# GpSimd's sums of exponentials added head by head, in an attention kernel with a mixture of experts

## The chip, the cores and the metric

The kernel runs on one core of a Trainium2 chip. The metric is the device time of one execution, in microseconds. The core has five engines that the text names: TensorE (PE in the profile; PEld is its loading of weights), VectorE (DVE), ScalarE (ACT), GpSimd (POOL) and SyncE (SP, which here only issues DMAs). Each takes its own instructions strictly in order, and semaphores hold an instruction until what it needs is there.

## What is computed

Attention with a capped score, in float32, over 8 batches, 12 heads, 448 positions and 64 columns a head. Then each of the 3584 tokens goes to one of 8 experts, of which each keeps the 80 tokens with the largest gate weight:

```python
scores = cap * np.tanh(scale * np.matmul(q, k.transpose(0, 1, 3, 2)) / cap)
attn = np.exp(scores - scores.max(-1, keepdims=True))
attn = attn / (attn.sum(-1, keepdims=True) + 1e-09)
x = np.matmul(attn, v)                      # -> (3584, 768)
expert_idx = np.argmax(x @ w_gate, axis=1)  # gate_w: its softmax probability
# per expert e: the `capacity` tokens of largest gate_w
out[tok] = gate_w[tok, None] * (np.maximum(x[tok] @ w1[e], 0.0) @ w2[e])
```

## The kernel before

The attention loop takes the heads in pairs, 48 of them (6 a batch). The scores of a pair lie with the 448 keys on partitions, in chunks of 128, and the 448 queries along the free axis. `qk` (L1033) multiplies a chunk for both heads into a PSUM tile sc (L1047) and ScalarE takes its tanh into the tile e (L1055). `expo` (L1057) takes the exponential in place (L1060). `av` (L1066) multiplies the exponentials with the values (L1071), four heads at a time; L1090 and L1100 add the 64 keys that are left over.

The denominator needs the sum of the exponentials over the keys. `esum` (L1103), the function that is changed, adds chunks on GpSimd: L1108 adds the second chunk to the first for both heads, 896 columns, into the tile t1 (the trace calls it t), and L1110 adds the third. `sums` (L1112) then lets TensorE sum over the partitions: in a group of two pairs, four matmuls read t (L1117) and four read the keys left over (L1118), into the PSUM tile sp. VectorE transposes sp (L1121, into st), adds a guard (L1123), takes the reciprocal (L1124) and spreads it (L1126, into r). `scaled` (L1129) multiplies av by r into x (L1133), which frees av's PSUM bank for the next group. `turned` (L1135) transposes x into xb (L1141), which GpSimd's queue stores once a batch (L1147). `swap` (L1074) exchanges the halves of the left-over keys (L1082).

The order is written out by hand: the strings EVEN, ODD, NEXT and LAST (L52 to L55) name the steps of a pair. q is `qk`, x and y are `expo` with `esum` right behind it, a is `av`, u is `sums`, n is `scaled`, m is `turned`, w is `swap`. At each b the function `background` (L1237) puts in some of the gate's and the ranking's work, which is mostly VectorE's, by costs that are written beside each piece. None of these costs or strings is touched.

The names in the background work that matter here: `gate_math` (L283) finds each token's expert and its key, with w at L322 and g at L336; `ranks` (L392) compares the keys of all tokens, with gb at L425 (L420 in the end), gl at L411, and the TensorE sums pd (L432), which VectorE adds into dfc (L438) and so frees a PSUM bank of the tag misc that sp shares. `prune` (L524) keeps the first candidates after five batches, with r at L543, us at L559, prlh at L566, prov at L573 and prrh at L576. `order` (L242), the other function that is changed, puts the experts that have tokens first: o1 makes a key, o4 the list as integers, from which SyncE later takes the addresses of the weights. `one` (L238) is tensor_scalar in the form that also writes out a sum, here into a place that nobody reads.

Behind the loop the tokens chosen are fetched and go through six experts (L779), while SyncE loads the weights (L767) into buffers, most of which lie where the loop's tiles were.

Of the kernel before, what the change touches and what calls it, by code (L numbers as in the profile page):

```python
# [12 lines left out]
ALU = mybir.AluOpType  # L13
# [21 lines left out]
NPRE = 4  # L35
# [86 lines left out]
def attn_moe(ctx, tc, q2, k, v, cap, wg, w1, w2, capacity, ct, out):  # L122
    nc = tc.nc
# [25 lines left out]
    def cst(key, n=128):  # L149
        a, b = CT[key]  # L150
        return ctt[:n, a:b]
# [24 lines left out]
    ev = consts.tile([128, E], F32, name="ev")  # L176
    ev0_i = consts.tile([1, NPRE], I32, name="ev0_i")
# [10 lines left out]
    neso = consts.tile([128, E], F32, name="neso")  # L188
# [43 lines left out]
    def wide(a, n=E):  # L232
        return a.rearrange("p (a e) -> p a e", a=1).broadcast_to([a.shape[0], n, E])

    def deep(a, n=E):
        return a.rearrange("p (e a) -> p e a", a=1).broadcast_to([a.shape[0], E, n])

    def one(dst, src, s=0.0, op=ALU.add):  # L238

        nc.vector.tensor_scalar(dst, src, s, 0.0, op0=op, op1=ALU.add, accum_out=dump[:dst.shape[0]])  # L240

    def order(sm):  # L242

        key = sm.tile([128, E], F32, name="okey", tag="okey")
        pos = sm.tile([128, E], F32, name="opos", tag="opos")
        pm = sm.tile([128, E, E], F32, name="opm", tag="opm")

        def o1():
            nc.vector.tensor_scalar(key, neso, 0.0, 8.0, op0=ALU.is_equal, op1=ALU.mult)
            nc.vector.tensor_tensor(key, key, cst("io"), op=ALU.add)  # L250

        def o2():
            t = sm.tile([128, E, E], F32, name="ocmp", tag="ocmp")
            nc.vector.tensor_tensor(t, wide(key), deep(key), op=ALU.is_lt)
            nc.vector.tensor_reduce(pos, t, axis=AX.X, op=ALU.add)
            nc.vector.tensor_tensor(pm, wide(pos), deep(cst("io")), op=ALU.is_equal)

        def o3(dst, key):
            t = sm.tile([128, E, E], F32, name="ocmp2", tag="ocmp")
            nc.vector.tensor_tensor(t, pm, wide(key), op=ALU.mult)  # L260
            nc.vector.tensor_reduce(dst, t, axis=AX.X, op=ALU.add)

        def o4():
            nc.vector.tensor_copy(ev0_i, ev[0:1, 0:NPRE])
            nc.vector.tensor_scalar(rev, ev, -1.0, float(E), op0=ALU.mult, op1=ALU.add)
            nc.vector.tensor_tensor(gtv, wide(ev), deep(ev), op=ALU.is_gt)
            st["ordered"] = True
        return [o1, o2] + [lambda d=d, k=k: o3(d, k) for d, k in ((ev, cst("io")), (powv, cst("pow")), (nesk, neso))] + [o4]
# [726 lines left out]
    with ExitStack() as a2:  # L995
# [107 lines left out]
        def esum(p, i):  # L1103
            s = st[p]
            e = s["e"]
            if i == 0:
                t1 = s["es"] = sm.tile([CK, 2, S], F32, name=f"t1{p}", tag="t1", bufs=3)
                nc.gpsimd.tensor_tensor(t1, e[:, 0:2], e[:, 2:4], op=ALU.add)  # L1108
            else:
                nc.gpsimd.tensor_tensor(s["es"], s["es"], e[:, 4:6], op=ALU.add)  # L1110

        def sums(u):  # L1112

# [185 lines left out]
        for t in range(n + 1):  # L1299
# [12 lines left out]
            if 1:  # L1312
# [3 lines left out]
                for i, x in enumerate(todo):  # L1316
# [3 lines left out]
                    if k_ == 'q' and t < n:  # L1320
                        qk(t, a_)
                    elif k_ == 'q' and t == n:
                        begin()
                    elif k_ == 'x' and t < n:
                        expo(t, 0, 2)
                        esum(t, 0)
                    elif k_ == 'y' and 1 <= t <= n:
                        expo(t - 1, 2, 4)
                        esum(t - 1, 1)
                    elif k_ == 'a' and 2 <= t < n + 2:  # L1330
                        av((t - 2) // 2, int(x[1]), int(x[2]))
                    elif k_ == 'w' and t >= 2:
                        swap(t // 2 - 1)
                    elif k_ == 'l' and t >= 3:
                        av_late((t - 3) // 2 if t < n else (n - 2) // 2)
                    elif k_ == 'u' and (t % 2 and 3 <= t < n or t == n):
                        sums((t - 2) // 2)
                    elif k_ == 'n' and 3 <= t:
                        for f in range(2):
                            scaled((t - 3) // 2 if t < n else (n - 2) // 2, f)  # L1340
                    elif k_ == 'm' and t >= 4:
                        normed((t - 4) // 2)
                    elif k_ == 'b' and t < n + 2:
                        share = sum(c for c, _, _ in bg + urgent) / (PLACES * (left - 1) + todo[i:].count('b'))
                        share += sum(c for c, _, _ in low) / max(1, PLACES * (n - 2 - t))
                        background(min(max(share, 600), 2200 if t < LATER else 3500 if t < n else 4500), 0, SLACK[t >= LATER][t % 2][todo[:i].count('b')] if t < n else TAIL)
# [146 lines left out]
```

## Time and profile before

| | us |
|---|---|
| runs | 496.76 (median), 493.79, 499.2 |
| profiled execution, time | 499.33 |
| profiled execution, span of the trace | 497.5 |
| TensorE busy | 462.9 (93%) |
| ScalarE busy | 343.9 (69%) |
| VectorE busy | 281.7 (57%) |
| GpSimd busy | 263.1 (53%) |
| GpSimd's additions at L1108, 48 | 101.2 |
| GpSimd's additions at L1110, 48 | 101.0 |

The span runs from the first to the last instruction of the program; the time has 1.8 us around it. The granted clock of TensorE is 0.985 of full speed over the span. The loop takes about the first 377 us. An idle time in brackets behind an instruction is that of its engine just before it, with what ended it by the profile; where several semaphores are waited for, the profile names the one that came last among those it can see.

### The profile page before, as it was taken

The numbers are of one execution on the slowest core, as the hardware profiler recorded it, in microseconds if no ns is written. First come the engines' busy times: TensorE is split into PE (matmuls) and PEld (weight loads), VectorE is DVE, ScalarE is ACT, GpSimd is POOL, SyncE is SP. The second block draws the span as 40 slices with busy tenths as digits, with TensorE's granted clock in tenths as the row PEclk, the third lists the DMA queues.
The fourth block names the chain that finished last, engine by engine and source line by source line (L and its number), as shares of the span: only waits on it lengthen the run. The fifth ranks groups of instructions, "written<-read, shape, count | busy, mean of one in ns | idle before, by whom it ended". The sixth has DMA issues, their size and how long they took to land.

```text
span 497.5 us, 15023 instructions
## 1 busy us (share of the span) xinstructions
PE 462.9 (93%) x6188; PEld 208.0 (42%) x6188; DVE 281.7 (57%) x772; ACT 343.9 (69%) x370; POOL 263.1 (53%) x201
## 2 busy tenths in 40 slices
PE   6899999999989999989999989989999889979894
PEld 1122232232323332323333323324336778878793
DVE  1144447837784686498569938895676523433000
ACT  4999989989978997896888857885964044601111
POOL 1666676666557656565755673566494237224001
PEclk9999999999999999999999989999999989899998
DMA  5557478758737875753676475578269999999901
GB/s 152 150 155 214 115 187 226 217 149 231 165 83 185 209 220 151 173 159 112 167 204 165 119 209 135 127 201 219 65 189 376 343 393 387 319 352 349 347 8 48
DMA packets 68111, 99.14 MB, mean 199 GB/s; under 512 B 19232, under 2 KB 53056, under 8 KB 68032
## 3 DMA queue, kind: packets, MB, share of 16 engines
q1 hardware_dynamic: 63360, 83.82, 55.6%
q0 software_dynamic: 4672, 14.26, 11.3%
q8 instruction: 51, 0.84, 0.7%
q14 instruction: 28, 0.23, 0.1%
HBM read 74.54 MB, written 23.51 MB: 197 GB/s over the span
## 4 chain that ended last, share of the span: by engine, by line
PE 83%; DVE 8%; issue 3%; ACT 3%; POOL 1%; DMA 1%; SPq 0%; POOLq 0%; DVEq 0%; ACTq 0%
PE sc L1047 22%; PE av L1071 21%; PE hp L779 9%; PE yt L779 8%; PE sp L1117 4%; PE sp L1118 3%; PE sc L1054 3%; PE av L1100 3%; PE lgp L1160 3%; PE av L1090 2%; PE pd L432 2%; ACT e L1055 2%; ACT e L1060 1%; DVE gl L411 1%; PE yp L800 1%
## 5 line engine op out<-in xcount | busy, mean ns | idle before, releaser
L1055 ACT ACTIVATE e<-sc,scl 128x896 f32<-128x896 f32 x168 | 161.7, 1007 | 57.3 <-PE sc L1047 55.5
L1060 ACT ACTIVATE e<-e,capt 128x1792 f32<-128x1792 f32 x96 | 153.8, 1603 | 0.0
L1108 POOL TENSOR_TENSOR t<-e 128x896 f32<-128x896 f32 x48 | 101.2, 2109 | 89.2 <-ACT e L1060 89.1
L1047 PE MATMUL sc<-qt,kt 64*64 64x448 f32 x1152 | 134.4, 563 | 7.1 <-DMA qt<-in_q_dram 4.7
L1071 PE MATMUL av<-e,vr 128*32 128x448 f32 x1152 | 132.4, 545 | 4.1 <-DVE x L1133 4.1
L1110 POOL TENSOR_TENSOR t<-t,e 128x896 f32<-128x896 f32 x48 | 101.0, 2103 | 57.2 <-ACT e L1060 49.0
L1047 PEld LDWEIGHTS sc<-qt,kt 64*64 64x64 f32 x1152 | 35.7, 134 | 89.8 <-ACT e L1055 40.0
L1071 PEld LDWEIGHTS av<-e,vr 128*32 128x32 f32 x1152 | 33.3, 109 | 81.3 <-issue 62.1
L779 PE MATMUL yt<-thv,w 128*64 128x80 f32 x1152 | 45.3, 237 | 6.5 <-issue 6.5
L779 PE MATMUL hp<-xt,w 128*64 128x80 f32 x1152 | 45.5, 239 | 5.8 <-issue 5.0
L1082 DVE TENSOR_SCALAR_CACHE_REDUCE sw<-e 64x896 f32<-64x896 f32 x32 | 34.6, 1080 | 25.3 <-ACT e L1060 24.9
L779 PEld LDWEIGHTS hp<-xt,w 128*64 128x64 f32 x1152 | 42.8, 141 | 8.7 <-issue 7.4
L779 PEld LDWEIGHTS yt<-thv,w 128*64 128x64 f32 x1152 | 42.7, 140 | 8.0 <-issue 7.6
L1121 DVE STREAM_TRANSPOSE st<-sp 128x448 f32<-128x448 f32 x24 | 15.5, 648 | 53.4 <-PE sp L1118 53.3
L1133 DVE TENSOR_TENSOR x<-av,r 128x448 f32<-128x448 f32 x48 | 27.9, 619 | 22.9 <-PE av L1100 21.0
L425 DVE TENSOR_SCALAR_CACHE_REDUCE gb<-krow,kc 112x896 bf16<-112x896 f32 (+8 forms) x37 | 31.8, 882 | 0.0
L823 POOL DMA_INDIRECT out_dram<-ysv,si x6 | 5.7, 944 | 45.7 <-ACT ysv L822 32.3
L423 ACT ACTIVATE gz<-gb 112x896 bf16<-112x896 bf16 (+12 forms) x22 | 18.5, 844 | 13.8 <-DVE gb L420 13.7
L1141 DVE STREAM_TRANSPOSE xb<-x 128x448 f32<-128x448 f32 x48 | 27.9, 619 | 0.0
L1117 PE MATMUL sp<-t,ones 128*32 128x448 f32 x192 | 24.3, 567 | 3.8 <-POOL t L1108 2.2
L411 DVE SCALAR_TENSOR_TENSOR gl<-krow,kc,ctt 112x112 bf16<-112x112 f32 x32 | 27.6, 862 | 0.0
L1118 PE MATMUL sp<-e,half 128*32 128x448 f32 x192 | 23.8, 556 | 0.0
(230 smaller groups left out, 402.7 us busy)
## 6 DMA issues: line engine op xcount, KB each, us to landing
w<-in_w_dram SPq DMA_DIRECT2D x36, 512.0 KB, 6.1
w<-in_w_dram SPq DMA_DIRECT2D x48, 384.0 KB, 5.7
kt<-in_k_dram SPq DMA_DIRECT2D x96, 112.0 KB, 2.9
qt<-in_q_dram SPq DMA_DIRECT2D x96, 112.0 KB, 2.8
xs<-xb POOLq DMA_DIRECT2D x28, 336.0 KB, 6.9
vr<-in_v_dram SPq DMA_DIRECT2D x40, 192.0 KB, 3.1
out_dram<-zero SPq DMA_DIRECT2D x4, 1536.0 KB, 8.4
out_dram<-zero SPq DMA_DIRECT2D x4, 1152.0 KB, 5.5
```

Of the source, the lines that this page charges most:

```text
L411: nc.vector.scalar_tensor_tensor(g, krow[:, x:x + C], kp, cst("tri", C), op0=ALU.is_equal, op1=ALU.mult, accum_out=acc[:, nk + c, 1:2])
L425: nc.vector.tensor_scalar(g, krow[:, x:y], kp, 0.0, op0=ALU.is_ge, op1=ALU.add, accum_out=a)
L779: nc.tensor.matmul(ps[j // per][64 * h:64 * h + 64, j % per * m:(j % per + 1) * m], w[:, 128 * j + 64 * h:128 * j + 64 * h + 64], x[:, kk, ...
L1047: nc.tensor.matmul(ps[KR * i:KR * i + KR, h, :S], s["k"][w, x:x + KR], s["q"][w], start=True, stop=True)
L1055: nc.scalar.activation(s["e"][:, 2 * c:2 * c + 2], ps[:, :, :S], AF.Tanh, scale=scl)
L1060: nc.scalar.activation(x, x, AF.Exp, scale=capt)
L1071: nc.tensor.matmul(st["av", u, f][32 * g:32 * g + 32, :S], st[p]["v"][:, g % 2, c, 32 * f:32 * f + 32], st[p]["e"][:, 2 * c + g % 2], star ...
L1082: nc.vector.tensor_scalar(o[w], x[KR * (1 - a):KR * (1 - a) + KR, 2 * NK:2 * NK + 2], 1.0, 0.0, op0=ALU.mult, op1=ALU.add, accum_out=dump[w])
L1108: nc.gpsimd.tensor_tensor(t1, e[:, 0:2], e[:, 2:4], op=ALU.add)
L1110: nc.gpsimd.tensor_tensor(s["es"], s["es"], e[:, 4:6], op=ALU.add)
L1117: nc.tensor.matmul(sp[32 * g:32 * g + 32, :S], ones[:, 0:32], s["es"][:, g % 2, :], start=True, stop=False)
L1118: nc.tensor.matmul(sp[32 * g:32 * g + 32, :S], half[:, g % 2 ^ g // 2], late(2 * u + g // 2), start=False, stop=True)
```

## The change

`esum` issues two instructions where it had one, at both places: the columns of the first head, then those of the second. In `order`, o1 compares first in the form with an accumulator and then multiplies and adds in one operation with two tensor inputs, and o4 makes the integers in the form with an accumulator.

```diff
@@ order
         def o1():
-            nc.vector.tensor_scalar(key, neso, 0.0, 8.0, op0=ALU.is_equal, op1=ALU.mult)
-            nc.vector.tensor_tensor(key, key, cst("io"), op=ALU.add)
+            one(key, neso, 0.0, ALU.is_equal)
+            nc.vector.scalar_tensor_tensor(key, key, 8.0, cst("io"), op0=ALU.mult, op1=ALU.add)
...
         def o4():
-            nc.vector.tensor_copy(ev0_i, ev[0:1, 0:NPRE])
+            one(ev0_i, ev[0:1, 0:NPRE])
             nc.vector.tensor_scalar(rev, ev, -1.0, float(E), op0=ALU.mult, op1=ALU.add)
             nc.vector.tensor_tensor(gtv, wide(ev), deep(ev), op=ALU.is_gt)
@@ esum
                 t1 = s["es"] = sm.tile([CK, 2, S], F32, name=f"t1{p}", tag="t1", bufs=3)
-                nc.gpsimd.tensor_tensor(t1, e[:, 0:2], e[:, 2:4], op=ALU.add)
+                for h in range(2):
+                    nc.gpsimd.tensor_tensor(t1[:, h], e[:, h], e[:, 2 + h], op=ALU.add)
             else:
-                nc.gpsimd.tensor_tensor(s["es"], s["es"], e[:, 4:6], op=ALU.add)
+                for h in range(2):
+                    nc.gpsimd.tensor_tensor(s["es"][:, h], s["es"][:, h], e[:, 4 + h], op=ALU.add)
```

GpSimd's queue at the start of the loop, for the first two pairs (t is t1, e a pair's exponentials, and behind each row stand the engines that it waits for). Before:

```order
L1108 TENSOR_TENSOR t_236<-e_216 128x896 [waits Activation_49]
L1110 TENSOR_TENSOR t_236<-t_236,e_216 128x896 [waits Activation_49,Pool_49]
L1108 TENSOR_TENSOR t_276<-e_248 128x896 [waits Activation_49]
L1110 TENSOR_TENSOR t_276<-t_276,e_248 128x896 [waits Activation_49,Pool_49]
L1108 TENSOR_TENSOR t_319<-e_288 128x896 [waits Activation_49]
```

Changed (L1109 and L1112 are the lines that were L1108 and L1110):

```order
L1109 TENSOR_TENSOR t_236<-e_216 128x448 [waits Activation_49]
L1109 TENSOR_TENSOR t_236<-e_216 128x448
L1112 TENSOR_TENSOR t_236<-t_236,e_216 128x448 [waits Activation_49,Pool_49]
L1112 TENSOR_TENSOR t_236<-t_236,e_216 128x448 [waits Pool_49]
L1109 TENSOR_TENSOR t_278<-e_249 128x448 [waits Activation_49]
L1109 TENSOR_TENSOR t_278<-e_249 128x448
L1112 TENSOR_TENSOR t_278<-t_278,e_249 128x448 [waits Activation_49,Pool_49]
L1112 TENSOR_TENSOR t_278<-t_278,e_249 128x448 [waits Pool_49]
```

The second half of each addition stands right behind the first and waits for no other engine.

TensorE's queue at the first group of sums (ones and half are constants, sp the PSUM tile). Before:

```order
L1117 MATMUL sp_358<-t_236,ones 32x448 [waits DVE_49,Pool_49]
L1118 MATMUL sp_358<-e_248,half 32x448
L1117 MATMUL sp_358<-t_236,ones 32x448
L1118 MATMUL sp_358<-e_248,half 32x448
L1117 MATMUL sp_358<-t_276,ones 32x448 [waits Pool_49]
L1118 MATMUL sp_358<-e_248,half 32x448
L1117 MATMUL sp_358<-t_276,ones 32x448
```

Changed (L1119 and L1120 were L1117 and L1118):

```order
L1119 MATMUL sp_364<-t_236,ones 32x448 [waits DVE_49,Pool_49]
L1120 MATMUL sp_364<-e_249,half 32x448
L1119 MATMUL sp_364<-t_236,ones 32x448 [waits Pool_49]
L1120 MATMUL sp_364<-e_249,half 32x448
L1119 MATMUL sp_364<-t_278,ones 32x448 [waits Pool_49]
L1120 MATMUL sp_364<-e_249,half 32x448
L1119 MATMUL sp_364<-t_278,ones 32x448 [waits Pool_49]
```

The matmuls stand where they stood; each of the four that read t now waits for its own half.

VectorE's queue at the expert order, in the fifth batch's ranking (okey is the key, neso the counts of tokens). Before:

```order
L425 TENSOR_SCALAR gb_17_3085,acc<-krow,kc 112x896 x2
L249 TENSOR_SCALAR okey<-neso 128x8
L250 TENSOR_TENSOR okey<-okey,ctt 128x8
L425 TENSOR_SCALAR gb_17_3085,acc<-krow,kc 112x224
L411 SCALAR_TENSOR_TENSOR gl_17_3141,acc<-krow,kc,ctt 112x112
```

Changed:

```order
L425 TENSOR_SCALAR gb_17_3157,acc<-krow,kc 112x896 x2
L240 TENSOR_SCALAR okey,dump<-neso 128x8
L250 SCALAR_TENSOR_TENSOR okey<-okey,ctt 128x8
L425 TENSOR_SCALAR gb_17_3157,acc<-krow,kc 112x224
L411 SCALAR_TENSOR_TENSOR gl_17_3215,acc<-krow,kc,ctt 112x112
```

The two operations keep their place, and what stands around them is the same.

## Rows read from the trace of the kernel before

**Rows 1.** Windows: length; busy us of PE, PEld, DVE, ACT, POOL; clock; DMA share

```profile
226.00:289.00 63.00, 63.00 (x672) 20.15 (x669) 51.61 (x125) 52.55 (x50) 36.80 (x21) 1.00 0.57 154
377.00:497.50 120.50, 100.96 (x2524) 94.51 (x2518) 34.61 (x134) 31.41 (x70) 35.18 (x56) 0.95 0.79 289
```

**Rows 2.** Timeline ahead of the first gap: start, us, engine, line, [idle before]

```profile
129.51 0.33 DVE L411 SCALAR_TENSOR_TENSOR gl<-krow,kc,ctt 112x112 bf16<-112x112 f32 x1
...
132.26 2.10 POOL L1108 TENSOR_TENSOR t<-e 128x896 f32<-128x896 f32 x1 [2.88 <-ACT e L1060]
132.28 2.21 DVE L411 SCALAR_TENSOR_TENSOR gl<-krow,kc,ctt 112x112 bf16<-112x112 f32 x1
...
136.04 2.11 POOL L1110 TENSOR_TENSOR t<-t,e 128x896 f32<-128x896 f32 x1 [1.68 <-ACT e L1060]
...
136.49 1.79 DVE L411 SCALAR_TENSOR_TENSOR gl<-krow,kc,ctt 112x112 bf16<-112x112 f32 x1
...
140.84 0.98 PE L1117 MATMUL sp<-t,ones 128*32 128x448 f32 x8 [1.60 <-DVE dfc L438]
```

**Rows 3.** Timeline ahead of the second gap, by engine

```profile
211.45 2.11 POOL L1110 TENSOR_TENSOR t<-t,e 128x896 f32<-128x896 f32 x1 [1.47 <-ACT tau L305]
...
221.80 2.08 POOL L1108 TENSOR_TENSOR t<-e 128x896 f32<-128x896 f32 x1 [2.83 <-ACT e L1060]
...
212.07 1.53 DVE L322 TENSOR_TENSOR w<-tau,rd 112x32 f32<-112x32 f32 x1
...
214.46 1.75 DVE L336 TENSOR_SCALAR g<-g 112x4 f32<-112x4 f32 x1
...
222.23 1.77 DVE L411 SCALAR_TENSOR_TENSOR gl<-krow,kc,ctt 112x112 bf16<-112x112 f32 x1
...
224.60 0.68 PE L1071 MATMUL av<-e,vr 128*32 128x448 f32 x4 [2.32 <-DVE x L1133]
```

**Rows 4.** Timeline ahead of the third gap

```profile
322.85 2.06 DVE L543 SCALAR_TENSOR_TENSOR r<-prov,r 112x20 f32<-112x20 f32 x1
...
325.60 2.12 POOL L1108 TENSOR_TENSOR t<-e 128x896 f32<-128x896 f32 x1 [0.74 <-ACT e L1060]
...
326.04 1.73 DVE L559 TENSOR_TENSOR us<-us,prpay 112x20 f32<-112x20 f32 x1
...
327.90 4.18 DVE L566 TENSOR_TENSOR prlh<-r,ctt 112x768 bf16<-112x768 f32 x3
...
328.43 2.37 POOL L1110 TENSOR_TENSOR t<-t,e 128x896 f32<-128x896 f32 x1 [0.71 <-ACT e L1060]
...
335.99 1.81 PE L1071 MATMUL av<-e,vr 128*32 128x448 f32 x16 [1.78 <-DVE x L1133]
```

**Rows 5.** Timeline at the fourth gap, ScalarE and TensorE

```profile
294.04 0.52 ACT L1170 COPY lgs<-lgp 96x448 f32<-96x448 f32 x1
...
294.66 1.75 PE L1117 MATMUL sp<-t,ones 128*32 128x448 f32 x8 [2.21 <-POOL t L1108]
```

**Rows 6.** Timeline at the loop's end, by engine

```profile
368.05 1.11 DVE L425 TENSOR_SCALAR_CACHE_REDUCE gb<-krow,kc 112x880 bf16<-112x880 f32 x1
...
369.08 1.64 DVE L411 SCALAR_TENSOR_TENSOR gl<-krow,kc,ctt 112x112 bf16<-112x112 f32 x1
...
370.65 2.77 DVE L420 TENSOR_SCALAR gb<-krow,kc 112x896 bf16<-112x896 f32 x2
...
368.48 2.11 POOL L1108 TENSOR_TENSOR t<-e 128x896 f32<-128x896 f32 x1
370.67 2.09 POOL L1110 TENSOR_TENSOR t<-t,e 128x896 f32<-128x896 f32 x1
...
373.56 0.97 PE L1117 MATMUL sp<-t,ones 128*32 128x448 f32 x8
```

**Rows 7.** Groups by line and form on GpSimd: count, busy us, mean ns

```profile
L1108 POOL TENSOR_TENSOR t<-e 128x896 f32<-128x896 f32 x48 | 101.2, 2109 | 89.2 <-ACT e L1060 89.1
...
L491 POOL TENSOR_TENSOR fpos<-fcmp 128x8 f32<-128x8 f32 x1 | 0.2, 202 | 0.1
```

## The prediction

> **What bounds the kernel now.** I first looked, stretch by stretch, at where TensorE stands still, because it is the engine that the chain of waits runs on for most of the span. In the attention loop it is full: the 63 us from 226 on hold 63.00 us of its work [rows 1]. So an edit on GpSimd or VectorE is worth only what it takes out of TensorE's gaps. After the first few microseconds the loop has four gaps: 1.60 us before 140.84 [rows 2], 2.32 before 224.60 [rows 3], 1.78 before 335.99 [rows 4] and 2.21 before 294.66 [rows 5], 7.91 us together. That is the most that this change can win there, 1.6% of the span. In the expert stage behind the loop TensorE has 101 us of work in 120.5, and the DMA engines are 0.79 busy [rows 1].
>
> Then I asked what VectorE does ahead of the gaps. The first gap ends with VectorE's dfc, the second and third with its x. In each run-up, operations that are short elsewhere last until a GpSimd addition ends. gl takes 0.33 us when GpSimd is idle, but 2.21 when it starts 0.02 behind an addition, which ends at 134.36 with gl ending at 134.49 [rows 2]. The operations held this way have two inputs in SBUF (gl, w, us, prlh) or are a plain tensor_scalar (L336). Operations in the accumulator form (L425) run through an addition unharmed: the one at 368.05 spans the start of L1108 and takes its usual 1.1 us [rows 6]. So VectorE and GpSimd exclude each other for whole instructions, and one GpSimd instruction is 2.1 us long.
>
> **The change, part by part.** 96 additions of 896 columns become 192 of 448. The trace has no addition of 448 columns, so I take a line through 896 columns, 2.109 us, and 8 columns, 0.202 us [rows 7]: 2.148 ns a column and 0.185 us fixed, so 1.15 us for a half and 2.30 for a pair. The bounds are 1.05 (half of 2.109, nothing fixed) and 1.25 (the fixed part paid more than one and a half times). I take 1.15, as both rows are the same operation on the same engine. Each addition grows by 0.19 us, 18 us over the program. That alone costs nothing, as GpSimd mostly waits for ScalarE's exponential before an addition (2.88, 1.68, 2.83 us in [rows 2, 3]). Without that cover it would be 0.19 us an addition.
>
> What the halves give depends on VectorE getting in between them. [Rows 6] bear on that: gl, held since 369.08, ends at 370.72, 0.13 after L1108, although L1110 was ready behind it. And L420 right after had to wait for L1110. So the two take turns, and a turn is now 1.15 us instead of 2.1. The Trainium skill (SBUF — State Buffer, section Who interferes with whom) states the same lock: whoever issues first has the shared ports for a whole instruction and the other blocks fully. By that rule the first half's end frees the port, and the sum is the one below. It doesn't say who is next when both want it, and these rows are what I have on that.
>
> Gap one. L1108 begins at 132.26, so its first half ends at 133.41 and gl at 133.54 instead of 134.49, 0.95 sooner. Up to the second gl VectorE has no other wait, so that gl starts at 135.54 instead of 136.49. The second half is over by 134.6 and L1110 begins at 136.04, as ScalarE sets it. So gl is free, takes 0.33 and ends at 135.87 instead of 138.28: 2.41 us sooner. dfc follows without a further wait, and TensorE was ready 1.60 us before it came. The gap goes: -1.60. The margin is 0.8 us, but gl passes 0.2 us ahead of L1110.
>
> Gap two. w at 212.07 ends at 212.63 instead of 213.60. The second half then holds the next two-input operation until 213.8, so L336 comes only 0.3 us sooner, at 214.2. It ended at 216.21, with an L1108 that by its 2.1 us must have begun at 214.08; the first half lets L336 go at 215.25, 0.95 sooner. VectorE works on without idling to gl, now at 221.28 instead of 222.23. L1108 starts at 221.80, so gl is through at 221.6 instead of 224.00, 2.4 sooner. x was the last wait by 2.32. The gap goes: -2.32. The margins are 0.1 and 0.2 us.
>
> Gap three. Here most of VectorE's chain wants the port. r (L543, held from 322.85) ends at 323.95, 0.95 sooner. But the second half holds the first us until 325.1, the other us ends at about 325.6, just as L1108 comes, and the next L1108 half holds the first prlh until 326.75. The three prlh took 4.18 us, of which some 1.9 is L1110 (328.43 to 330.80), so about 0.9, 0.9 and 0.5 are their own. Now each finds another half in front of it, L1108's second, then both of L1110: one ends at 327.65, two at 329.5, three at 331.0 instead of 332.08, and L1110's second half then holds prov behind them until 332.1. What is saved at the beginning is handed back in turns, since GpSimd's additions have to pass through the same chain. I take -0.1, between -1.78 (VectorE wins the ties) and +1.1 (one more half gets in).
>
> Gap four stays. The row names L1108, but the sums there read earlier pairs; ScalarE's copy of lgp into lgs ends at 294.56 [rows 5], and the bank that it frees is what fits. The change leaves ScalarE's order alone: 0.
>
> The sums. sp now waits for each half (four waits in eight matmuls instead of two), and the last half lands 0.19 us later, more where VectorE slips in. At the loop's end, four halves from 368.48 take 4.60, and the two L420 use the port for about 0.66 (2.77 less the 2.1 of L1110), so the last lands at 373.74 where sp began at 373.56 [rows 6]: +0.2. Other groups have their additions well behind them.
>
> The expert order. L249 gets the accumulator form and isn't held, but the operation behind it now has two tensor inputs and a scalar, the form of r and gl, which are held. So the wait only moves to it. At L264 the plain tensor_scalar L265 behind it inherits the wait. Both stand in the stretch from 226 to 289, where TensorE is full [rows 1]: 0. Without that cover they would cost or give at most one addition, 2.1 us.
>
> The sum is -1.60 - 2.32 - 0.1 + 0.2 = -3.82 us on the profiled execution: 499.33 becomes 495.5. That execution lies 2.57 above the median of the three runs, 496.76. The gaps come from a fixed order on each engine, so I take the same 3.82 off the median: **492.9**.
>
> **The rivals.** *All three gaps go.* VectorE wins two ties around 325.6 and prlh comes out a half earlier: -1.60 - 2.32 - 1.78 + 0.2 = -5.5, 491.3. For it: the tie at 325.6 is within 0.1 us. Against it: from there on both engines want the port without a pause.
>
> *A tie is lost in gap one or two.* L1108 or L1110 takes the port just ahead of gl, which waits 1.15 us more. In gap two 1.2 of the 2.32 stay; in gap one the margin still covers most. Saving 2.6: 494.2.
>
> *VectorE is not let in at the seam.* The pair then acts as one instruction of 2.30, each held operation waits 0.19 longer, and nothing is saved. Eight such waits ahead of the three gaps (two, three, three) give +1.5: 498.3. Against it: gl at 370.72 [rows 6].
>
> *The sums come late* (the other side). Every VectorE operation that gets between halves puts off the rest. The last group's addition ends 0.8 us before sp; once 0.19 plus the operations let in exceed a group's lead, TensorE stands. At 0.3 us (one gl) in each of 24 groups that is +7.2, less 4.05 won: 499.9. Against it: most groups have a ScalarE wait, not a full queue, ahead of the addition.
>
> *The gain is lost behind the loop.* If the weight transfers set the end from a start of their own, the time stays 496.8. Against it: their buffers are freed by the loop's last work, so they should move with it.
>
> **How the numbers follow.** Chances: forecast 0.44, all three 0.18, a lost tie 0.16, no seam 0.07, late sums 0.09, lost behind 0.06. Runs shown of one kernel lie 493.79 to 499.2, so about 1% (5 us) is what a measurement of this kernel can tell from no change. Faster by over 1% means below 491.8: most of the second case and a third of the first, 0.33. Slower by over 1%, above 501.7, is left to part of the late sums and what I missed: 0.08. Within 1%: 0.59. The range reaches from all three gaps with a point of spread to the rival without a seam: 489.8 to 497.8; the forecast's own is 491.3 to 494.2.
>
> **What would show it.** In the changed profile: halves of 1.15 us; gl (L411) nowhere above about 1.5 us, where it reaches 2.2 now; no TensorE gap around 140 and 223; the gap near 335 still there at 1.5 to 1.9; the one near 294 unchanged; the two okey operations trading the wait. Wrong it would be if gl still takes 2.2, if sp waits for GpSimd in many groups, or if the loop ends 4 us sooner and the program doesn't.

## The result, and the profile after

| | before | after |
|---|---|---|
| median of 14 runs each, us | 498.55 (493.79 to 501.44) | 491.95 (488.17 to 494.5) |
| profiled execution, time / span, us | 499.33 / 497.5 | 493.09 / 491.3 |
| granted clock over the span | 0.985 | 0.990 |
| VectorE busy, us | 281.7 | 270.0 |
| GpSimd busy, us | 263.1 | 278.1 |

The ratio of after to before is 0.9878 (95% interval 0.9855 to 0.9902): 6.1 us faster (4.9 to 7.2 by the interval), 1.2%; between the two medians lie 6.6 us. The forecast was 492.9, from a median of 496.76; more runs of the kernel before have put that median 1.8 higher, so the gain is 6.1 where 3.82 was forecast, and it falls into "faster by over 1%", which had a chance of 0.33. Here and below, ratios and means leave out the runs that lie more than 1.5% above the fastest of their kernel: one of 29 of the kernel before in the third set of experiments (1143 us), one of 6 with halves for the first pairs, two of 6 of the kernel without gaps (with them its ratio would be 0.976) and two of 12 with halves at gap one (with them its mean clock would be 0.9786, below the 0.9796 of the kernel before).

The additions of the changed kernel by line and form (count, then busy us and mean ns, then idle time ahead of them), against [rows 7]:

```profile
L1109 POOL TENSOR_TENSOR t<-e 128x448 f32<-128x448 f32 x96 | 108.8, 1156 | 78.0 <-ACT e L1060 77.9
L1112 POOL TENSOR_TENSOR t<-t,e 128x448 f32<-128x448 f32 x96 | 108.7, 1153 | 49.0 <-ACT e L1060 41.4 <-ACT tau L305 5.7 <-ACT neso L281 1.9
```

A half takes 1.15 us, as the line through [rows 7] said. GpSimd is 15 us busier for it, 0.16 an addition, a little less than the 0.19 foretold: two queued halves overlap by 0.04 us, so a pair takes 2.27.

TensorE in the stretches of gaps one and two (windows; first length and TensorE's busy us):

```profile
130.00:142.00 12.00, 12.00 (x135) 3.78 (x123) 10.06 (x26) 10.74 (x10) 7.81 (x7) 1.00 0.48 129
203.00:226.00 23.00, 23.00 (x248) 6.69 (x240) 19.03 (x53) 21.98 (x22) 13.52 (x12) 1.00 0.61 168
```

Both are full now. All that TensorE waits for in the loop after the first 25 us (waits: what waits, for what, us in all, times, the longest):

```profile
PE sp L1119 <- POOL t L1109: 2.2, 1, 2.2
PE av L1071 <- DVE x L1135: 1.4, 1, 1.4
PE hp L779 <- DVE xt L626: 0.3, 1, 0.3
```

Of the four gaps two are left, the fourth with its 2.2 us and the third with 1.4 instead of 1.78. The 0.3 us are new: an expert's first matmuls, which stand at the loop's end, wait for tokens fetched.

**Gap one**, timelines of VectorE, GpSimd and TensorE, against [rows 2]:

```profile
131.94 1.26 DVE L411 SCALAR_TENSOR_TENSOR gl<-krow,kc,ctt 112x112 bf16<-112x112 f32 x1
...
135.20 0.33 DVE L411 SCALAR_TENSOR_TENSOR gl<-krow,kc,ctt 112x112 bf16<-112x112 f32 x1
...
131.93 2.28 POOL L1109 TENSOR_TENSOR t<-e 128x448 f32<-128x448 f32 x2 [2.72 <-ACT e L1060]
135.71 2.25 POOL L1112 TENSOR_TENSOR t<-t,e 128x448 f32<-128x448 f32 x2 [1.50 <-ACT e L1060]
...
138.83 0.98 PE L1119 MATMUL sp<-t,ones 128*32 128x448 f32 x8
```

The first gl starts 0.01 us behind a pair of halves, as it did behind a whole addition, and is through at 133.20, 0.12 after the middle of the pair (131.93 + 1.15). So it got in at the seam, the point between two queued halves. The second is ahead of L1112 by half a microsecond, and free. sp has no idle time ahead of it.

**Gap two**, against [rows 3]:

```profile
210.06 0.57 DVE L322 TENSOR_TENSOR w<-tau,rd 112x32 f32<-112x32 f32 x1
...
210.98 0.73 DVE L326 SCALAR_TENSOR_TENSOR kc<-u,wsc 112x4 f32<-112x4 f32 x1
...
212.06 0.17 DVE L336 TENSOR_SCALAR g<-g 112x4 f32<-112x4 f32 x1
...
218.26 0.33 DVE L411 SCALAR_TENSOR_TENSOR gl<-krow,kc,ctt 112x112 bf16<-112x112 f32 x1
...
209.44 2.25 POOL L1112 TENSOR_TENSOR t<-t,e 128x448 f32<-128x448 f32 x2 [1.34 <-ACT tau L305]
212.07 2.28 POOL L1109 TENSOR_TENSOR t<-e 128x448 f32<-128x448 f32 x2 [0.38 <-ACT e L1060]
```

w (1.53 before) ends at the first half's end, kc at the second's. L336, which was held for 1.75, now starts 0.01 us ahead of the next pair and isn't held at all.

**Gap three**, against [rows 4]:

```profile
318.48 0.95 DVE L543 SCALAR_TENSOR_TENSOR r<-prov,r 112x20 f32<-112x20 f32 x1
...
320.10 0.44 DVE L559 TENSOR_TENSOR us<-us,prpay 112x20 f32<-112x20 f32 x1
...
321.14 5.14 DVE L566 TENSOR_TENSOR prlh<-r,ctt 112x768 bf16<-112x768 f32 x3
326.21 1.27 DVE L573 TENSOR_TENSOR prov<-rev,cms 112x160 bf16<-112x160 f32 x1
...
321.09 2.96 POOL L1109 TENSOR_TENSOR t<-e 128x448 f32<-128x448 f32 x2 [0.59 <-ACT e L1060]
324.01 3.28 POOL L1112 TENSOR_TENSOR t<-t,e 128x448 f32<-128x448 f32 x2
...
331.15 1.81 PE L1071 MATMUL av<-e,vr 128*32 128x448 f32 x16 [1.44 <-DVE x L1135]
```

r and us are won as in the other gaps (2.06 to 0.95, 1.73 to 0.44), and then the three prlh take 5.14 instead of 4.18: each finds a half in front of it, and each pair of halves is stretched to 2.96 and 3.28 by the prlh between. prov behind them takes 1.27, where the kernel before has

```profile
332.01 0.31 DVE L573 TENSOR_TENSOR prov<-rev,cms 112x160 bf16<-112x160 f32 x1
```

That is the giving back in turns.

**Gap four**, against [rows 5], and the loop's end, against [rows 6]:

```profile
289.51 0.52 ACT L1172 COPY lgs<-lgp 96x448 f32<-96x448 f32 x1
...
290.13 1.28 PE L1119 MATMUL sp<-t,ones 128*32 128x448 f32 x8 [2.21 <-POOL t L1109]
```

```profile
364.70 4.11 DVE L411 SCALAR_TENSOR_TENSOR gl<-krow,kc,ctt 112x112 bf16<-112x112 f32 x1
...
364.24 2.24 POOL L1109 TENSOR_TENSOR t<-e 128x448 f32<-128x448 f32 x2
366.44 2.23 POOL L1112 TENSOR_TENSOR t<-t,e 128x448 f32<-128x448 f32 x2
...
369.06 0.97 PE L1119 MATMUL sp<-t,ones 128*32 128x448 f32 x8
```

Gap four is the old one to the hundredth. At the loop's end one gl is not let in at three seams in a row and lasts 4.11 us, longer than any operation of this form before. It ends when GpSimd's queue of halves does. Nothing on TensorE waits for it, and the last sp starts 0.4 us after the last half.

In the spans, 6.2 us apart, the start holds 0.3 (the first sp is at 25.36 instead of 25.70), the loop from there to its last av 4.17 (346.92 instead of 351.09), which is the gaps' 1.60 + 2.32 + 0.34 less 0.1, and the stretch behind it 1.7 (119.0 instead of 120.75). That last part varies from 118.1 to 120.8 among these two profiles and those of the first set of experiments, with and without halves (119.6 with the small operations alone), so it is not credited to the change. Then 4.2 us of gaps stand against 6.1 us of time, and the experiments had to look for the rest.

### The profile page after: what moved, and what is told of

Read it like the earlier page. It is cut to its first block, busy times and chain, and to the rows that moved or that the text cites. A ratio compares the mean times of both kernels' runs of the same rounds, so it can differ in the third digit from the quotient of the medians.

```text
span 491.3 us, 15122 instructions
## 1 busy us (share of the span) xinstructions
PE 460.4 (94%) x6188; PEld 206.3 (42%) x6188; DVE 270.0 (55%) x774; ACT 343.9 (70%) x370; POOL 278.1 (57%) x297
## 3 DMA queue, kind: packets, MB, share of 16 engines
q0 software_dynamic: 4672, 14.26, 11.5%
## 4 chain that ended last, share of the span: by engine, by line
PE 76%; issue 8%; DMA 5%; DVE 4%; ACT 3%; POOL 3%; POOLq 0%; SPq 0%; DVEq 0%; ACTq 0%
PE sc L1047 23%; PE av L1071 22%; PE hp L779 6%; PE sp L1119 4%; PE sp L1120 4%; PE sc L1054 3%; PE yt L779 3%; PE av L1100 3%; PE lgp L1162 2%; DMA out_dram<-ysv,si 2%; PE pd L432 2%; PE av L1090 2%; ACT e L1055 2%; ACT e L1060 1%; DMA xge<-xs,gi 1%
## 5 line engine op out<-in xcount | busy, mean ns | idle before, releaser
L1109 POOL TENSOR_TENSOR t<-e 128x448 f32<-128x448 f32 x96 | 108.8, 1156 | 78.0 <-ACT e L1060 77.9
L1112 POOL TENSOR_TENSOR t<-t,e 128x448 f32<-128x448 f32 x96 | 108.7, 1153 | 49.0 <-ACT e L1060 41.4
L779 PE MATMUL yt<-thv,w 128*64 128x80 f32 x1152 | 43.7, 234 | 7.1 <-issue 7.1
L779 PEld LDWEIGHTS yt<-thv,w 128*64 128x64 f32 x1152 | 41.4, 137 | 8.4 <-issue 8.1
L1119 PE MATMUL sp<-t,ones 128*32 128x448 f32 x192 | 23.8, 556 | 2.2 <-POOL t L1109 2.2
L1120 PE MATMUL sp<-e,half 128*32 128x448 f32 x192 | 23.8, 556 | 0.0
L1149 POOL DMA_DIRECT2D xs<-xb x36 | 22.9, 643 | 0.0
```

What stands on the lines that cost most here:

```text
L779: nc.tensor.matmul(ps[j // per][64 * h:64 * h + 64, j % per * m:(j % per + 1) * m], w[:, 128 * j + 64 * h:128 * j + 64 * h + 64], x[:, kk, ...
L1109: nc.gpsimd.tensor_tensor(t1[:, h], e[:, h], e[:, 2 + h], op=ALU.add)
L1112: nc.gpsimd.tensor_tensor(s["es"][:, h], s["es"][:, h], e[:, 4 + h], op=ALU.add)
L1119: nc.tensor.matmul(sp[32 * g:32 * g + 32, :S], ones[:, 0:32], s["es"][:, g % 2, :], start=True, stop=False)
L1120: nc.tensor.matmul(sp[32 * g:32 * g + 32, :S], half[:, g % 2 ^ g // 2], late(2 * u + g // 2), start=False, stop=True)
```

## The experiments

Three sets ran on three chips, each beside the kernel before on its own chip (median 498.4, 506.42 and 506.13 us), so ratios are compared across sets and times only within one.

### One part alone: the halves, or the small operations

The halves alone are the change without the two edits in `order`; the other kernel is those two edits alone.

> The additions in halves alone; the two operations of the expert order as before. My theory (only TensorE's gaps count, and these two operations stand where TensorE is full): the same time as the whole change, about 0.988 of before, TensorE's gaps near 140 and 223 gone, the one near 331 at 1.4 us, the one near 290 at 2.2. Rival (the small operations matter, by what waits behind them): a part of the 6 us is missing, 0.990 to 1.0.

Ratio 0.9893 (0.9845 to 0.9941). The waits of TensorE from 130 to 340 us read as in the changed kernel: 2.2 for sp and 1.4 for av.

> The two operations of the expert order alone; the additions whole. My theory: no change, 0.997 to 1.003, all four gaps of TensorE as before (1.6, 2.3, 2.2, 1.8 us), and the second operation on okey lasts about 2 us in place of the first. Rival: 1 to 2 us faster, by an earlier list of experts and so earlier weights.

Ratio 1.0006 (0.9978 to 1.0035). All four gaps are there. VectorE's timeline at the expert order:

```profile
273.39 0.15 DVE L240 TENSOR_SCALAR_CACHE_REDUCE okey<-neso 128x8 f32<-128x8 f32 x1
...
273.59 1.83 DVE L250 SCALAR_TENSOR_TENSOR okey<-okey,ctt 128x8 f32<-128x8 f32 x1
```

In the kernel before, L249 stood there with 2.02 us and L250 with 0.17. The wait has moved by one operation and nothing else has. The whole effect is that of the halves.

### Halves for the first pairs, or the last

```diff
-                for h in range(2):
+                for h in (range(2) if p < 30 else [slice(0, 2)]):
```

The second kernel has p >= 30 there. Neither has the two edits in `order`.

> Halves in the first 30 pairs of heads only, which takes in the first two gaps (near 140 and 224 us) and neither the third nor the loop's end. Theory of the gaps: both gaps go, 3.9 us less up to the third gap, the third gap stays at 1.8, time about 0.992. Rival (a good part of the 6 us comes from behind the loop, since GpSimd's and VectorE's order at the loop's end changes): the loop ends 3.9 us sooner here, the stage behind it stays at 120.7 us from the last matmul on the values to the end, and e6_halves_last has the rest.

Ratio 0.988 (0.9841 to 0.992).

> Halves in the last 18 pairs only. Theory of the gaps: the first two gaps stay (1.6 and 2.3 us), the third goes from 1.8 to about 1.5, time within 0.5 us of before. Rival (gain behind the loop): 1.5 to 2 us less, seen as a stage of about 119 us from the last matmul on the values to the end, where before has 120.75.

Ratio 0.9988 (0.996 to 1.0016). TensorE's waits from 130 to 340 us, first with halves for the first pairs, then for the last:

```profile
PE sp L1119 <- POOL t L1109: 2.2, 1, 2.2
PE av L1071 <- DVE x L1135: 1.8, 1, 1.8
```

```profile
PE av L1071 <- DVE x L1135: 3.8, 2, 2.3
PE sp L1119 <- POOL t L1109: 2.2, 1, 2.2
PE sp L1119 <- DVE dfc L438: 1.6, 1, 1.6
```

Each gap follows the additions beside it: gaps one and two carry the gain, and the 18 pairs from 30 on bring only gap three's 0.34. The rival went by the stretch behind the loop, and in the profile of the second kernel that is 118.1 us, as it said (120.4 in the first). But with whole additions and the small operations it was 119.6, and the second kernel's runs show no gain; the upper end of theirs, 2 us, does not shut the rival out.

### The lock by form: gl with one tensor input

```diff
-            nc.vector.scalar_tensor_tensor(g, krow[:, x:x + C], kp, cst("tri", C), op0=ALU.is_equal,
-                                           op1=ALU.mult, accum_out=acc[:, nk + c, 1:2])
+            nc.vector.tensor_scalar(g, krow[:, x:x + C], kp, 0.0, op0=ALU.is_equal, op1=ALU.add, accum_out=acc[:, nk + c, 1:2])
```

> Whole additions as before, but gl (L411) takes one tensor input and keeps its accumulator: the count of equal keys is over the whole row and not only over the earlier columns (the mask tri is left out; the two accumulators start from -2 to make up for it), so ranks are the reference's only where no two keys are equal. My theory (the lock is by instruction form; the form of L425 in rows 6 is not held): gl takes about 0.3 us at every place, also beside a whole addition. Gap one goes (two gl, 1.88 and 1.46 us longer than 0.33, against a gap of 1.60). In gap two only gl's 1.44 are won, w and L336 stay held, so 0.9 of the 2.32 stay. Gaps three and four stay at 1.8 and 2.2. Together 3.0 us off: ratio 0.994 (0.991 to 0.997). Rival (what matters is the number of GpSimd instructions and their seams, not the form of gl): gl stays near 1.8 to 2.2 beside an addition, the gaps stay, ratio 1.000. If gaps one and two are all that the halves win, this kernel comes near the one with halves (0.988) without any change on GpSimd.

Ratio 0.9893 (0.9855 to 0.9931). All 32 gl by their shortest, median and longest ns (L413 here), and TensorE's waits from 130 to 340 us:

```profile
L413 DVE TENSOR_SCALAR_CACHE_REDUCE gl<-krow,kc x32: 285/324/332, 85.6 to 423.1; 112x112 bf16<-112x112 f32 x32
```

```profile
PE av L1072 <- DVE x L1134: 2.7, 2, 1.8
PE sp L1118 <- POOL t L1109: 2.2, 1, 2.2
```

The longest gl is 332 ns, beside whole additions of 2.1 us. Gap one is gone; gap two is 0.88 us, where 0.9 was expected (w and L336 are still held, 1.53 and 1.76); gaps three and four are untouched. So the lock goes by the form of VectorE's instruction, and a gap's price is the sum of the held operations ahead of it less TensorE's lead. The time fell by more than the 3.0 us of the gaps, though, 5.5, and the ratio lies below the 0.991 to 0.997 expected.

### Gap four: the copy of lgp on VectorE

```diff
-                nc.scalar.copy(st["lgs", b], st["lp", b][0:96, :S])
+                (nc.vector.tensor_copy if b == OB else nc.scalar.copy)(st["lgs", b], st["lp", b][0:96, :S])
```

> The changed kernel, with the copy of lgp into lgs of the second batch (L1172, the one ahead of the gap at 290) on VectorE instead of ScalarE, where it stands behind two score activations and an exponential. My theory (step on gap four: ScalarE's copy frees the bank that sp waits for): TensorE's gap of 2.21 us goes, and with it the drop of the granted clock to half that mostly follows it (some 1.6 us): 2.2 to 3.9 us off the changed kernel, ratio to the kernel before 0.980 to 0.984. Rival (the profile's own row: sp waits for GpSimd's addition L1109): the gap stays at 2.2 us or more, ratio 0.988 as with the changed kernel.

Ratio 0.9826 (0.9787 to 0.9864). VectorE's copy and TensorE's sums:

```profile
285.60 0.62 DVE L1172 COPY lgs<-lgp 96x448 f32<-96x448 f32 x1 [2.75 <-PE lgp L1162]
...
287.65 0.98 PE L1119 MATMUL sp<-t,ones 128*32 128x448 f32 x8
```

sp no longer waits. The profile put that gap down to GpSimd's t; but no addition was touched here, and the gap went with ScalarE's copy, so ScalarE's copy was what sp waited for, as the prediction read it (lgp and sp take their PSUM banks from the same pool of two).

### Smaller pieces: four of 224 columns

```diff
-                for h in range(2):
-                    nc.gpsimd.tensor_tensor(t1[:, h], e[:, h], e[:, 2 + h], op=ALU.add)
+                for h in range(4):
+                    w = slice(224 * (h % 2), 224 * (h % 2) + 224)
+                    nc.gpsimd.tensor_tensor(t1[:, h // 2, w], e[:, h // 2, w], e[:, 2 + h // 2, w], op=ALU.add)
```

(L1112 likewise.)

> The changed kernel with each addition in four pieces of 224 columns instead of two of 448. By the line of rows 7 a piece takes 0.67 us and a whole addition 2.66 (2.31 in halves, 2.11 whole), 34 us more of GpSimd over the program. My theory (the engines take turns, an instruction each, and the time only hangs on TensorE's gaps): gaps one and two stay gone; prlh, prov and prrh wait for a piece of 0.67 instead of 1.15 in front of each, so gap three shrinks from 1.44 to about 0.3 to 0.9; the sums still come in time, since the shortest lead in the changed kernel is 0.44 us at the third sum of the first group and 0.76 at the last, and a group's last addition grows by 0.35. Ratio 0.986 to 0.988 (0.5 to 1 us off the changed kernel). Rival (late sums decide): the longer additions use up the leads, sp waits for GpSimd in the first and last groups and in those with a lead near 1 us, 0.3 us or more each, and the ratio goes back to 0.990 or above.

Ratio 0.9872 (0.9834 to 0.991), not to be told from halves. The pieces by line and form, VectorE's chain at gap three, and all that TensorE waits for from 130 to 340 us:

```profile
L1110 POOL TENSOR_TENSOR t<-e 128x224 f32<-128x224 f32 x192 | 124.1, 679 | 62.5 <-ACT e L1060 62.0
```

```profile
318.82 3.23 DVE L566 TENSOR_TENSOR prlh<-r,ctt 112x768 bf16<-112x768 f32 x3
321.98 0.78 DVE L573 TENSOR_TENSOR prov<-rev,cms 112x160 bf16<-112x160 f32 x1
```

```profile
PE sp L1121 <- POOL t L1110: 2.2, 1, 2.2
```

A piece is 0.68 us (the line said 0.67), prlh falls from 5.14 to 3.23, and gap three is gone, more than expected. So the turns set that gap. The rival is in it too, once: the first group's eight matmuls of sp take 1.24 us where they take 0.98, because its last quarter lands at 24.91, 0.24 after sp began. What gap three gave is not seen in the time, whose interval is wider than that.

### Gap three from the other side: a different place in the queue

As the kernel with the copy on VectorE, and one number of the planner:

```diff
-            yield 900, lambda i=i: left(i), 0
+            yield 1800, lambda i=i: left(i), 0
```

> As the kernel with lgs on VectorE, and the planner's cost of one prlh step (left, three of them) set from 900 to 1800, which puts the last prlh, prov and prrh behind st, rc, r and the two x in VectorE's queue, and the prt matmuls that read them later in TensorE's. My theory (gap three is nothing but x queued behind a chain that is held in turns): TensorE no longer waits for x near 331, gap three goes from 1.44 to 0, ratio 0.977 to 0.980, about 1.4 us under the kernel that only has lgs moved. Rival (the chain is on the path by itself): prt now waits for prlh or prrh about as long as av waited for x, and the ratio is that of the kernel with lgs moved.

Ratio 0.9727 (0.9668 to 0.9787), and TensorE waits for nothing between 130 and 340 us. On its timeline prt, which reads prlh and prrh, comes last and finds them ready:

```profile
326.03 1.71 PE L1071 MATMUL av<-e,vr 128*32 128x448 f32 x16
...
330.23 1.07 PE L582 MATMUL prt<-prrh,prlh 112*96 112x40 bf16 x20
```

The chain was on the path only because x stood behind it. A new gap stands at the loop's end, where an expert's first matmuls wait at 358.9 for tokens fetched (waits from 25 to 372 us):

```profile
PE hp L779 <- DVE xt L626: 1.2, 1, 1.2
```

So 6.8 of the 7.91 us are gone. The ratio is below what was expected, with an interval that reaches into it; the runs scatter from 489.54 to 498.45. A part of the gain is not the gaps': the stretch behind the loop takes 121.8 us in this profile, and 124.9 to 126.6 in the other three of the chip, for a reason that no run shows. By its ratio this kernel beats both the one before and the changed one.

### Is the lock still worth anything without gaps?

The kernel without gaps with the short gl on top, and the same two edits on whole additions:

> The kernel with lgs on VectorE and left at 1800, which has none of the four gaps, and gl (L411) in the form with one tensor input on top (equal keys are counted over the whole row, so ranks are the reference's only where no two keys are equal). My theory (a held VectorE operation costs only what it takes out of a TensorE gap): gl is short everywhere and VectorE's busy time falls by several us, but no gap is left in the loop that hangs on it: the same time as without it on the same chip, ratio 0.971 to 0.978. Rival (VectorE's time counts by itself, or gl is on the path in the expert stage too): 2 us or more below that, ratio under 0.970.

Ratio 0.9804 (0.9768 to 0.9839). From 25 to 371 us VectorE is busy 224.19 us, where the kernel without the short gl has 228.79, and TensorE 344.50 against 344.11. The 4.6 us of VectorE bought nothing: the ratio's interval overlaps that of the kernel without the short gl, and lies above the rival's 0.970. The ratio is also above the 0.971 to 0.978 expected; the two kernels ran on different chips, and a difference of under 1% between them can't be read from that.

> The same two edits as in the kernel without gaps (lgs on VectorE, left at 1800) made on the kernel before, so whole additions. My theory (the gaps are independent and add up): gaps one and two stay at 1.6 and 2.3 us, as only the halves remove them; gap four goes by lgs and gap three by left; 4.0 us of gaps less and what drops followed gap four: ratio 0.986 to 0.990, about 1.2% above the kernel that has the halves too. Rival (with st and x ahead of the chain, whole additions reach other waits, or gap three comes back for prlh held by 2.1 us at a time): gap three of 1 us or more stays, ratio 0.991 or above.

Ratio 0.9919 (0.9885 to 0.9954). TensorE's waits from 130 to 340 us:

```profile
PE av L1071 <- DVE x L1133: 2.3, 1, 2.3
PE sp L1117 <- DVE dfc L438: 1.6, 1, 1.6
```

Gaps three and four are gone without any halves, and gaps one and two stay: each gap can be taken out without the others. The ratio lies above the 0.986 to 0.990 expected. In the profile two new gaps at the loop's end, 1.12 us ahead of hp at 363.24 and 0.43 ahead of av at 373.10, take back 1.55 of the 3.99 us.

### What the gaps leave open: the clock

In the profile of the kernel before, the granted clock is half (1.2 of 2.4 GHz) right after gap four. It is not so in every execution. Stretches of 3.4 to 3.6 us behind gap four and behind gap two, as windows: the kernel before and the changed one behind gap four, the small edits alone and halves for the last pairs behind gap two (the clock is the third number from the end):

```profile
294.66:298.20 3.54, 3.54 (x20) 1.33 (x24) 0.21 (x1) 0.00 (x0) 1.84 (x1) 0.52 0.79 203
```

```profile
290.13:293.60 3.47, 3.47 (x24) 1.31 (x24) 0.60 (x1) 0.00 (x0) 2.18 (x3) 0.58 0.83 213
```

```profile
223.48:226.98 3.50, 3.50 (x26) 1.15 (x27) 3.50 (x8) 0.64 (x1) 2.09 (x1) 0.53 0.66 165
```

```profile
224.40:227.80 3.40, 3.31 (x40) 1.44 (x44) 3.40 (x7) 0.87 (x2) 2.10 (x1) 1.00 0.55 157
```

The last two kernels have the same gap of 2.32 us, by the same additions; the clock fell in one execution and not in the other. Over the 14 profiles, of all the kernels here, it fell behind gap four in 6 of 10 that have the gap, behind gap two in 2 of 5 that have it at its full 2.32, and behind none of 16 gaps of 0.88 to 1.78 us. Some 3.4 us at half speed leave 1.7 us of work undone, and the time grows by nearly as much: the step from sp of one group to that of the next is 17.8 us across gap two with a drop, 16.3 without, and 13.8 without the gap.

Each run also comes with its mean granted clock, and so the sum can be made for the runs that have no profile. (1 - clock) x span is the work at full speed that was not granted. It is too high by a part that costs nothing: in every profile the clock also falls 2.4 to 4.5 us behind TensorE's last matmul, which puts 1.3 to 2.4 us into it. In the kernel before, TensorE has nothing more to do there (window, second number):

```profile
490.30:497.50 7.20, 0.01 (x1) 0.00 (x0) 0.61 (x1) 0.21 (x1) 0.91 (x1) 0.66 0.17 47
```

For the kernel before on the first chip, 23 runs have 0.9854 on average, 7.2 us; the halves alone, 6 runs, 0.9892, 5.3 us. (The changed kernel's 14 runs have 0.9890.) The table sets the gaps removed (less new ones at the loop's end) plus this difference against the difference of the mean spans, all in us:

| kernel | gaps removed | clock given back | sum | measured |
|---|---|---|---|---|
| halves alone | 4.3 | 1.9 | 6.2 | 5.6 |
| small operations alone | 0 | -1.1 | -1.1 | -0.4 |
| halves, first pairs | 3.9 | 1.1 | 5.1 | 5.8 |
| halves, last pairs | 0.3 | 0.3 | 0.7 | 0.8 |
| short gl | 3.0 | 2.9 | 5.9 | 5.5 |
| lgs on VectorE | 6.5 | 3.5 | 10.0 | 9.1 |
| quarters | 5.4 | 2.6 | 8.0 | 6.6 |
| no gaps | 6.8 | 3.5 | 10.3 | 14.0 |
| no gaps, short gl | 6.8 | 3.0 | 9.8 | 11.5 |
| no gaps three and four, whole additions | 2.4 | 0.6 | 3.0 | 4.5 |
| halves at gap one | 1.6 | 1.7 | 3.3 | 3.2 |
| halves at gap two | 2.3 | 2.0 | 4.4 | 4.0 |

(The mean of a few runs is uncertain by 0.4 to 1 us in the clock's column and by 0.5 to 1.5 in the last; in the third set the ratios give 0.4 to 1.6 us less than the last column.) With gaps and clock together eight of the twelve come within 1 us, and four are off by 1.4 to 3.7; by the gaps alone eleven fall short, by 0.5 to 7. So the times go with the clock. The table does not say where in the program the clock was higher, nor that the gaps did it.

For the loop the profiles settle it. Take the time from the first matmul of sp to the end of the last one on the values, less TensorE's gaps (of 0.25 us and more), less half of the time at half clock. That leaves 341.1 to 342.3 us in 13 of the 14 profiles, and 343.2 with quarters: 351.09 - 7.91 - 1.71 in the kernel before, 346.92 - 3.93 - 1.71 in the changed one, 344.88 - 3.65 - 0 with the halves alone. So gaps and drops of the clock are, to about 1 us, all that the loops differ in. And the changed kernel's profile owes nothing to the clock there: both lost 1.71 us in the loop, behind gap four. All the difference in their clocks lies behind the loop, where 5.85 us were not granted before ([rows 1], last line) and 3.03 after:

```profile
377.00:491.30 114.30, 94.51 (x2397) 88.66 (x2393) 30.24 (x121) 30.54 (x70) 34.02 (x55) 0.97 0.79 289
```

The last two rows of the table were made to find out which gap the clock goes with:

```diff
+                for h in (range(2) if 14 <= p < 20 else [slice(0, 2)]):
```

The second kernel has 24 <= p < 30 there.

> The kernel before, with the additions in halves for six pairs only, 14 to 19, which are the ones around gap one. So far the gaps removed explain 4.2 us of the changed kernel's 6.1, and the mean granted clock of its runs is higher (0.9890 against 0.9854 of the kernel before), which is worth some 1.8 us. My theory (a gap above 2 us lets the clock fall in some executions, a shorter one doesn't): gap one goes and gives its 1.6 us and nothing more; gaps two to four stay; the mean clock stays that of the kernel before on the same chip, within 0.0015; ratio 0.9968 (0.994 to 0.999). Rival (the 1.8 us come with any gap removed): clock 0.001 to 0.002 up, ratio 0.994 or below.

Ratio 0.9951 (0.9922 to 0.998); mean clock 0.9829 against 0.9796. Gap one is gone and the others stay, as expected, but the clock rose by 0.0033, where at most 0.0015 was expected.

> The kernel before, with the additions in halves for pairs 24 to 29 only, around gap two. My theory (gap two of 2.32 us lets the clock fall in some executions): the gap goes, 2.3 us, and with it drops of the clock worth 1 to 1.8 us on average; mean clock 0.002 to 0.0035 above the kernel before on the same chip; ratio 0.992 to 0.994. Rival (gap two costs its length and no more): clock as before within 0.0015, ratio 0.9953. The two kernels together should give what the kernel with halves for pairs below 30 gave, 0.988.

Ratio 0.9931 (0.9904 to 0.9959); mean clock 0.9836, 0.0040 up. That is as expected, and the two ratios together make the 0.988 of the halves for the first pairs. But gap one alone did nearly as much for the clock. So my theory, that only a gap above 2 us matters for the clock, is not borne out as an account of the runs, although no profile shows a drop behind gap one. Where in the runs without a profile the clock was low can't be seen; a share of it lies behind the loop in every profile (0.95 of full speed from 377 us on in [rows 1]), and a shift there would show in the same number. That stays open.

## Why the prediction was right, and where it was not

**The half, and the seam.** 1.15 us as worked out, and 15 us more for GpSimd where 18 were foretold. VectorE is let in between two queued halves: in the changed kernel at 18 of the 21 seams at which a held operation was waiting. By the rule of the Trainium skill (SBUF — State Buffer, section Who interferes with whom) the ports are locked for a whole instruction and so free at the first half's end; the trace agrees, gl ending 0.12 us after it in gap one. The rival without a seam is out.

**Gaps one and two** went, -1.60 and -2.32, by the steps foretold: gl through at the middle of the pair, w at the first half's end. One step in gap two was off in the harmless direction: L336 was to be held to the end of a half, and came 0.01 us ahead of it instead. No tie was lost there.

**Gap three** gave 0.34 where 0.1 was taken, inside the bounds of -1.78 and +1.1. The reason was right: r and us won 1.1 and 1.3 us, the three prlh gave 0.96 back and prov behind them another 0.96, and a short operation ahead of r the last 0.14. The quarters confirm it: with a turn of 0.68 the gap goes.

**Gap four** stayed at 2.21, and the kernel with VectorE's copy shows that the reading behind it was right.

**The sums** were to cost 0.2 at the loop's end and cost nothing, because the step that was to delay them failed: gl, at 364.70, was not let in between the halves, so these came one after the other (four in 4.43 us, 4.60 foretold). "The two take turns" is thus not a rule: it held at 18 seams and failed at three, all in this one gl.

**The expert order**: the waits moved to L250 and L265 as written, and cost nothing.

**The sum** is where the prediction fell short: -3.82, against -4.26 in gaps and -6.1 in time (4.9 to 7.2). Of the missing 2.3 us, 0.34 - 0.1 + 0.2 = 0.44 lie in the two terms above. The other 1.8 have no term in the sum: it priced a gap at its length and left out the clock. What the profiles show of that is a drop behind gap two in 2 of 5, worth 0.7 us on average (an estimate, 0.4 x 1.7), which goes with the gap. I could have seen that a gap can have such a tail: in [rows 5] the eight matmuls of sp behind gap four take 1.75 us, and 0.98 behind gap one in [rows 2]. That drop itself is not won, as gap four stays. The last 1.1 us are open. The mean clock of the changed kernel's runs is higher by more than that, 0.9890 against 0.9854, but in the two profiles the difference lies behind the loop, and no run shows that the gaps made it. The 4.26 and 0.7 make 5.0, just inside the interval.

The sign, the place and the mechanism held. That 491.95 comes within 1 us of the forecast 492.9 is in part luck: the median that it started from was 1.8 us too low and the gain, by the medians, 2.8 too small, and the two errors pull opposite ways. In the rival of late sums the gain to set against 7.2 is 1.60 + 2.32 + 0.1 = 4.02 and not 4.05, which changes no figure behind it.

## What to carry to other kernels

Here a long GpSimd addition held the VectorE operations that use two SBUF inputs or are a plain tensor_scalar until it ended. Cutting it in two cost 0.16 us and gave VectorE a seam, and giving the held operation the accumulator form with one tensor input freed it altogether (gl at most 0.33 us). Either was worth just what it took out of a gap of the engine that is the bound, so list that engine's waits first, and price each held operation in their run-ups. Behind a gap of 2 us look for a drop of the clock: it was there in 8 of 15 cases and cost 1.5 to 1.7 us each. Look at the mean granted clock of all runs, not only at the profiled one, but before crediting a change with it, find out where in the program it lies.

## What the runs showed of the hardware that was not expected

**Who is held, and who is not.** In the kernel before, 37 VectorE operations that read two SBUF tiles or are a plain tensor_scalar started while an addition had 0.15 us or more to go, and all 37 ended behind it (all 14 such gl among them). Of the operations with one of their two inputs in PSUM (x and dfc), 14 started so, and none was held: x took 0.58 to 0.63 us and dfc at most 0.18.

**Lost seams.** In the changed kernel a gl waited through three seams for 4.11 us; in the halves alone (362.76 to 367.27) and in the halves for the last pairs (368.56 to 372.83) the same gl did the same. In these three GpSimd did eight halves there without any idle time, the gl beside the last four. In the kernels with lgs on VectorE, with quarters and without gaps it waited 0.16 to 0.67 us for an exponential ahead of the last additions, and no seam was lost. An unbroken queue alone does not do it, since the four halves from 321.09 to 327.29 at gap three have no idle time either and let a prlh in at each of their three seams. Whether it is the length of the queue was not tried, and stays open.

**The clock falls in some executions only.** Behind the same gap of 2.2 to 2.3 us, in the same kernel text around it, the granted clock was half of full speed for some 3.4 us in 8 of 15 cases, and full in the other 7. What decides it stays open.
